# The length-64 sums of an inverse transform kept as unsplit 32-bit numbers, and their transposing product run on 32-bit operands

## The chip, the cores and the metric

The kernel runs on one core of a Trainium2 chip. The metric is device time in microseconds (us) of one execution. The time before is the median of 3 runs. Engines are called PE (TensorE), PEld (the weight loads of TensorE, a row of its own in the profile), DVE (VectorE), ACT (ScalarE), POOL (GpSimd) and SP (SyncE, which issues most DMAs).

## The reference

```python
X = np.fft.rfft(x, axis=1)                       # x: 8 x 2496 x 256, 32-bit
Yr = Xr @ w_r - Xi @ w_i + b_r                   # w: 256 x 256
Yi = Xr @ w_i + Xi @ w_r + b_i
Y  = sign(Y) * max(abs(Y) - 0.01, 0)             # real and imaginary part each
y  = np.fft.irfft(Y, n=2496, axis=1)             # 8 x 2496 x 256
...
logits = y @ w_gate + modality_bias[modality_id] # 8 experts, the largest logit takes the token
out = gate_w * (relu(y @ w1[e]) @ w2[e])         # w1: 256 x 1024, w2: 1024 x 256
```

The 8 batches of 2496 rows are 19968 tokens for the second part. Everything is 32-bit in and out.

## The kernel before

The length 2496 is written as 39 times 64. The forward transform sums over 39 (function s1), passes through DRAM, sums over 64 (s2), multiplies by the weights (mix), shrinks, and the inverse sums over 64 (is2) and then over 39 (is1). A batch has 10 **pairs** p of frequency indices k1; one pair is the work of s2, mix, shrink and is2 for two k1. After its 10 pairs a batch has 22 **pivots** j. A pivot takes three of the 64 positions, 120 columns (3 positions x 20 k1 x real and imaginary), and with TensorE turns channels-on-partitions into frequencies-on-partitions; the same product makes the gate logits, because its moving operand holds the identity (128 columns) and 16 columns of gate weights. is1 then sums over 39 and leaves the tokens in a tile x1, from which indirect DMAs (scatter, issued by POOL) sort them by expert. When all batches are done, the expert layers run tile by tile to the end.

TensorE is given operands of the kind fp32r throughout: a 32-bit number is rounded to a shorter one (hi), the rest is kept as a second one (lo), and a product is written as a sum of products of halves, for example hi*hi + lo*hi + hi*lo. So each value that TensorE reads later costs a rounding copy (ACT), a subtraction (DVE or POOL) and more than one product.

The order on PE, ACT, DVE and POOL is written out by hand: each engine executes its instructions in the order of the program text and waits at the head of its queue. In step p of a batch the text is: load and split for pair p+4 and p+3, s2 of pair p+2, mix and shrink of pair p+1, is2 of pair p, and one to three small steps of the routing of the batch before (lines 509 to 570, DVE above all). In the loop over j each step is: one scatter, one pivot, the is1 of the pivot two steps earlier, and in every other step one s1 chunk of the batch after the next (batches 0 to 5 only).

The names that matter: zh and zl (the sums over 64, hi and lo, one tile each for a whole batch), Zt (the difference before lo is made), pv (the moving operand of the pivot), ph and pl (the halves of what the pivot gives). In is2_pair there are two k1 per pair, and for each one ACT rounds into zh (line 380), DVE subtracts into Zt (line 381) and DVE adds the low part of the product into zl (line 389). PSUM tiles z_*, from which all three read, have two buffers; the tile of s2 has one, and DVE is its last reader (lines 314 and 315).

Of the kernel before, what the change touches and what calls it, by code (L numbers as in the profile page):

```python
# [9 lines left out]
F32 = mybir.dt.float32  # L10
F32R = mybir.dt.float32r
# [11 lines left out]
N1, N2, K1 = 39, 64, 20  # L23
D = 256
E = 8
# [5 lines left out]
PK = 3 * 2 * K1  # L31
# [96 lines left out]
class Attn:  # L128
# [65 lines left out]
    def consts_last(self):  # L194

        nc, I, cp = self.nc, self.I, self.cp
        st = self.w3.tile([128, 4 * D], F32, tag="ev", name="st_g")
        nc.sync.dma_start(st[:PK, :256], I["c_g"])
        ident = st[:, 256:384]
        nc.gpsimd.memset(ident, 0.0)  # L200
        nc.gpsimd.affine_select(out=ident, in_=ident, compare_op=ALU.not_equal, fill=1.0, base=0,
                                pattern=[[-1, 128]], channel_multiplier=1)
        gst = st[:, 384:384 + 2 * E].rearrange("p (c e) -> p c e", c=2)
        nc.sync.dma_start(gst, I["moe_w_gate"].rearrange("(c p) e -> p c e", p=128))
        yield
        self.g = self.cl.tile([PK, 2, 128], F32R, name="c_g")
        nc.vector.tensor_copy(self.g, st[:PK, :256].rearrange("p (h n) -> p h n", h=2))

        self.pv = self.cl.tile([128, 2, 144], F32R, name="pv")
        for c in range(2):  # L210
            io, go = (0, 128) if c == 0 else (16, 0)
            nc.vector.tensor_copy(self.pv[:, c, io:io + 128], ident)
            nc.vector.tensor_copy(self.pv[:, c, go:go + E], gst[:, c, :])
            nc.vector.tensor_sub(self.pv[:, c, go + E:go + 2 * E], gst[:, c, :], self.pv[:, c, go:go + E])


    def s1_load(self, b, u, end=None, eng=None):
# [144 lines left out]
    def is2_pair(self, b, p, parts):  # L362

        nc = self.nc
        if p == 0:
            self.zh = self.w1.tile([128, 2, N2, K1, 2], F32R, tag="zh", name=f"zh_{b}")
            self.zl = self.w1.tile([128, 2, N2, K1, 2], F32R, tag="zl", name=f"zl_{b}")
        out = []
        k1s = [(sh[:, i], sl[:, i]) for _, sh, sl in parts for i in range(sh.shape[1])]
        for i, (sh, sl) in enumerate(k1s):  # L370
            k1 = 2 * p + i
            ps = self.ps.tile([128, 2, 256], F32, tag="z", name=f"z_{b}_{k1}")
            mv = self.q[:, k1 * 256:(k1 + 1) * 256]
            for c in range(2):
                nc.tensor.matmul(ps[:, c, :], sh[:, c * 128:(c + 1) * 128], mv, start=True, stop=False)
                nc.tensor.matmul(ps[:, c, :], sl[:, c * 128:(c + 1) * 128], mv, start=False, stop=True)
            hv = ps[:, :, 0:128].rearrange("p c (n r) -> p c n r", r=2)
            lv = ps[:, :, 128:256].rearrange("p c (n r) -> p c n r", r=2)
            t = self.w2.tile([128, 2, N2, 2], F32, tag="Zt", name=f"Zt_{b}_{k1}")
            nc.scalar.copy(self.zh[:, :, :, k1, :], hv)  # L380
            nc.vector.tensor_sub(t, hv, self.zh[:, :, :, k1, :])
            out.append((k1, t, lv))
            if len(parts) > 1:
                self.z_low(*out.pop())
        for o in out:
            self.z_low(*o)

    def z_low(self, k1, t, lv):
        self.nc.vector.tensor_add(self.zl[:, :, :, k1, :], t, lv)


    def pivot(self, b, j):
        nc = self.nc
        base = min(3 * j, N2 - 3)
        tag = "y" if j % 2 and (j < 16 or b >= self.nb - 2) else "z"
        ps = self.ps.tile([128, 512], F32, tag=tag, name=f"pv_{b}_{j}")
        first = True
        for c in range(2):
            for z in (self.zh, self.zl):
                lhsT = z[:, c, base:base + 3, :, :].rearrange("p n k r -> p (n k r)")  # L400
                nc.tensor.matmul(ps[:PK, c * 128:c * 128 + 144], lhsT, self.pv[:, c, :],
                                 start=first, stop=(c == 1 and z is self.zl), skip_group_check=True)
                first = False
        ph = self.w2.tile([PK, GC], F32R, tag="ph", name=f"ph_{b}_{j}")
        pl = self.w2.tile([PK, GC], F32R, tag="pl", name=f"pl_{b}_{j}")
        nc.scalar.copy(ph, ps[:PK, :GC])  # L406
        nc.vector.tensor_sub(pl, ps[:PK, :GC], ph)  # L407
        return ph, pl
# [839 lines left out]
```

## Time and profile before

| | |
|---|---|
| time, median of 3 runs | 1660.69 us (1658.56 to 1667.56) |
| the profiled execution: time | 1657.9 us |
| its span from first to last instruction | 1656.1 us |
| mean granted TensorE clock | 0.979 of full speed |
| busy: PE / PEld / DVE / ACT / POOL | 1566.3 / 1522.0 / 900.6 / 792.0 / 638.0 us |
| pairs and pivots of all batches | until about 713 us |
| expert layers | from about 714 us to the end |

Busy time is a sum of the durations of one engine's instructions, where overlapping ones count once. Matmuls are pipelined: the duration of one (some 0.27 us) is longer than the distance to the next one, so what a product costs a full PE is read from the distance between two starts. A "[idle before <-releaser]" note names what the engine waited for last; where the named engine was done long before, it was another.

### The profile page before, as it was taken

The page shows a single profiled execution, that of the slowest core. Times are in us where ns is not written, and L with a number is a line of the kernel's source. Part 1 is how long each engine was busy: PE and PEld are TensorE (multiplying, and loading weights), DVE is VectorE, ACT ScalarE, POOL GpSimd, SP SyncE. Part 2 cuts the span into 40 slices and gives each one's busy share as a digit, 9 for nine tenths or more (in the row PEclk, how much of TensorE's full clock was granted, in tenths as well). Part 3 has the DMA queues.
Part 4 walks back from the last instruction along what each step waited for, and adds up shares of the span by engine and source line. Part 5 has one row for each costly group of instructions (what it writes and reads, how often), then busy time and mean ns, then how long its engine had stood idle before and what let it go on. Part 6 is the DMA issues. An engine that isn't in the chain of part 4 may idle for free. (4 is left out here: it accounts for less than half of the span.)

```text
span 1656.1 us, 34047 instructions
## 1 busy us (share of the span) xinstructions
PE 1566.3 (95%) x12771; PEld 1522.0 (92%) x12771; DVE 900.6 (54%) x1847; ACT 792.0 (48%) x1658; POOL 638.0 (39%) x601
## 2 busy tenths in 40 slices
PE   4899989899989999999999999999999999999998
PEld 2788888798888888899999999999999999999998
DVE  3988978797979797754333333333333333333332
ACT  3678877787778776642322332323222332232232
POOL 1563767676767677621531111111111111111111
PEclk7999999999999999999999999999999999999999
DMA  7757575757475746551341411641114117515240
GB/s 204 253 165 233 163 249 160 243 162 251 150 243 161 228 141 207 173 202 40 94 129 51 158 41 41 256 147 40 53 54 145 40 54 299 202 41 219 78 151 20
DMA packets 120462, 246.18 MB, mean 149 GB/s; under 512 B 18890, under 2 KB 74262, under 8 KB 116479
## 3 DMA queue, kind: packets, MB, share of 16 engines
q1 hardware_dynamic: 101305, 201.78, 37.5%
q0 software_dynamic: 18992, 42.22, 7.6%
q8 instruction: 102, 1.67, 0.4%
q14 instruction: 63, 0.52, 0.1%
HBM read 433.83 MB, written 100.82 MB: 323 GB/s over the span
## 5 line engine op out<-in xcount | busy, mean ns | idle before, releaser
L869 POOL DMA_INDIRECT out<-o,ix x161 | 158.6, 985 | 750.9 <-ACT o L848 699.4
L856 PE MATMUL y<-w,hh 128*128 128x256 f32 x2496 | 433.6, 278 | 0.0
L826 PE MATMUL h<-xh,w 128*128 128x256 f32 x2496 | 425.6, 283 | 0.9 <-ACT xh L805 0.7
L856 PEld LDWEIGHTS y<-w,hh 128*128 128x128 f32 x2496 | 378.0, 188 | 0.4
L826 PEld LDWEIGHTS h<-xh,w 128*128 128x128 f32 x2496 | 346.0, 189 | 1.2 <-ACT xh L805 0.9
L856 PE MATMUL y<-w,hl 128*128 128x256 f32 x1248 | 346.6, 278 | 0.0
L829 DVE SCALAR_TENSOR_TENSOR hl<-h,hh 128x512 fp32r<-128x512 f32 x312 | 215.8, 692 | 230.2 <-ACT hh L828 230.1
L828 ACT ACTIVATE hh<-h 128x512 fp32r<-128x512 f32 x312 | 186.5, 598 | 272.0 <-PE h L826 272.0
L826 PE MATMUL h<-xl,w 128*128 128x256 f32 x1248 | 247.3, 280 | 0.2 <-DVE xl L806 0.2
L856 PEld LDWEIGHTS y<-w,hl 128*128 128x128 f32 x1248 | 234.4, 188 | 0.0
L846 DVE TENSOR_SCALAR o<-y,xt 128x256 f32<-128x256 f32 x78 | 37.7, 484 | 342.9 <-ACT o L848 338.6
L848 ACT ACTIVATE o<-y,xt 128x256 f32<-128x256 f32 x78 | 37.0, 474 | 360.6 <-PE y L856 360.6
L575 POOL DMA_INDIRECT xs<-x,si x176 | 180.2, 1024 | 54.8 <-issue 52.1
L826 PEld LDWEIGHTS h<-xl,w 128*128 128x128 f32 x1248 | 191.1, 189 | 0.4 <-DVE xl L806 0.4
L346 PE MATMUL mx<-wmix,Xh 128*128 128x256 f32 x1280 | 175.9, 281 | 0.0
L346 PEld LDWEIGHTS mx<-wmix,Xh 128*128 128x128 f32 x1280 | 162.0, 191 | 0.8 <-ACT mx L326 0.2
L296 POOL TENSOR_TENSOR al<-a,ah 128x512 fp32r<-128x512 f32 x80 | 109.5, 1369 | 74.5 <-ACT ah L295 48.1
L360 POOL TENSOR_TENSOR sl<-s,sh 128x512 fp32r<-128x512 f32 x77 | 100.1, 1300 | 85.3 <-ACT sh L359 72.4
L307 PE MATMUL s<-c_m,ah 128*128 128x256 f32 x320 | 83.5, 295 | 29.7 <-DVE Xl L315 10.6
L407 DVE TENSOR_TENSOR pl<-pv,ph 120x272 fp32r<-120x272 f32 x176 | 76.8, 439 | 53.4 <-ACT ph L406 46.3
L346 PE MATMUL mx<-wmix,Xl 128*128 128x256 f32 x640 | 100.2, 279 | 0.0
L307 PEld LDWEIGHTS s<-c_m,ah 128*128 128x128 f32 x320 | 61.8, 193 | 37.1 <-ACT zh L380 12.3
(199 smaller groups left out, 2830.0 us busy)
## 6 DMA issues: line engine op xcount, KB each, us to landing
w<-wsp SPq DMA_DIRECT2D x166, 2048.0 KB
xt<-xs SPq DMA_DIRECT2D x78, 272.0 KB
a<-scr SPq DMA_DIRECT2D x80, 256.0 KB
scr<-ev SPq DMA_DIRECT2D x112, 160.0 KB
x<-in_x SPq DMA_DIRECT2D x108, 156.0 KB
wr<-in_moe_w SPq DMA_DIRECT2D x64, 256.0 KB
wsp<-wh SPq DMA_DIRECT2D x64, 256.0 KB
wsp<-wl SPq DMA_DIRECT2D x64, 256.0 KB
```

Source lines behind the costliest of these rows:

```text
L296: nc.gpsimd.tensor_sub(al, at, ah)
L307: nc.tensor.matmul(o, ah[:, i, c * 128:(c + 1) * 128], mv, start=True, stop=False)
L346: self.nc.tensor.matmul(ps[i][:, i, :], t[:, 2 * i + c, o:o + 128], self.w[:, wi, c, lo, :], start=False, stop=n == len(ops) - 1, skip_gro ...
L360: eng.tensor_sub(sl, s, sh)
L407: nc.vector.tensor_sub(pl, ps[:PK, :GC], ph)
L575: i = self.nc.gpsimd.indirect_dma_start(out=self.xs, out_offset=bass.IndirectOffsetOnAxis(ap=si[:, k:k + 1], axis=0), in_=self.at.x1[:, j, ...
L826: nc.tensor.matmul(ps[:, q, :], w1[:, lo, c, f * 128:(f + 1) * 128], x[:, c, :], start=n == 0, stop=n == 5)
L828: nc.scalar.activation(hh[:, 2 * p:2 * p + 2, :], ps, AF.Relu)
L829: nc.vector.scalar_tensor_tensor(hl[:, 2 * p:2 * p + 2, :], ps, 0.0, hh[:, 2 * p:2 * p + 2, :], ALU.max, ALU.subtract)
L846: nc.vector.tensor_scalar_mul(o[:, s, :], y[s], gate)
L856: nc.tensor.matmul(y[s], lhsT, w2[:, lo, f, :], start=n == 0, stop=n == 23)
L869: ins = self.nc.gpsimd.indirect_dma_start(out=self.out, out_offset=bass.IndirectOffsetOnAxis(ap=ix, axis=0), in_=o, in_offset=None, bounds ...
```

## The change

The sums over 64 are stored as one unsplit 32-bit tile z instead of zh and zl: ACT copies the high columns of the product, DVE adds the low columns in place. The pivot multiplies z and pv as 32-bit operands (F32 instead of F32R), two products per pivot instead of four. pv holds the gate weights unsplit, and the 8 columns that held their low parts hold zeros. What follows the pivot (ph, pl, is1) stays.

```diff
-        self.pv = self.cl.tile([128, 2, 144], F32R, name="pv")
+        self.pv = self.cl.tile([128, 2, 144], F32, name="pv")
+        nc.vector.memset(self.pv, 0.0)
         for c in range(2):
...
-            nc.vector.tensor_sub(self.pv[:, c, go + E:go + 2 * E], gst[:, c, :], self.pv[:, c, go:go + E])
...
         if p == 0:
-            self.zh = self.w1.tile([128, 2, N2, K1, 2], F32R, tag="zh", name=f"zh_{b}")
-            self.zl = self.w1.tile([128, 2, N2, K1, 2], F32R, tag="zl", name=f"zl_{b}")
-        out = []
+            self.z = self.w1.tile([128, 2, N2, K1, 2], F32, tag="zh", name=f"z_{b}")
...
-            t = self.w2.tile([128, 2, N2, 2], F32, tag="Zt", name=f"Zt_{b}_{k1}")
-            nc.scalar.copy(self.zh[:, :, :, k1, :], hv)
-            nc.vector.tensor_sub(t, hv, self.zh[:, :, :, k1, :])
-            out.append((k1, t, lv))
-            if len(parts) > 1:
-                self.z_low(*out.pop())
-        for o in out:
-            self.z_low(*o)
-
-    def z_low(self, k1, t, lv):
-        self.nc.vector.tensor_add(self.zl[:, :, :, k1, :], t, lv)
+            z = self.z[:, :, :, k1, :]
+            nc.scalar.copy(z, hv)
+            nc.vector.tensor_add(z, z, lv)
...
-        first = True
         for c in range(2):
-            for z in (self.zh, self.zl):
-                lhsT = z[:, c, base:base + 3, :, :].rearrange("p n k r -> p (n k r)")
-                nc.tensor.matmul(ps[:PK, c * 128:c * 128 + 144], lhsT, self.pv[:, c, :],
-                                 start=first, stop=(c == 1 and z is self.zl), skip_group_check=True)
-                first = False
+            lhsT = self.z[:, c, base:base + 3, :, :].rearrange("p n k r -> p (n k r)")
+            nc.tensor.matmul(ps[:PK, c * 128:c * 128 + 144], lhsT, self.pv[:, c, :],
+                             start=c == 0, stop=c == 1, skip_group_check=True)
```

## Rows read from the trace of the kernel before

**Rows 1.** The page: span, and busy time, share and instructions of each engine.

```profile
span 1656.1 us, 34047 instructions
PE 1566.3 (95%) x12771; PEld 1522.0 (92%) x12771; DVE 900.6 (54%) x1847; ACT 792.0 (48%) x1658; POOL 638.0 (39%) x601
```

**Rows 2.** Windows, pairs of batch 2 and sum over batches 1 to 7: busy, clock, DMA.

```profile
226.00:282.00 56.00, 51.35 (x420) 49.46 (x421) 51.09 (x105) 45.10 (x98) 39.90 (x35) 1.00 0.57 179
...
sum 369.50, PE 343.94 PEld 332.70 DVE 334.02 ACT 296.49 POOL 258.89; mean PE 49.13 PEld 47.53 DVE 47.72 ACT 42.36 POOL 36.98
```

**Rows 3.** Windows, pivot loops of batches 0, 4 and 7 (of 8): the same columns.

```profile
117.50:143.50 26.00, 24.58 (x182) 22.67 (x183) 21.10 (x45) 21.46 (x56) 0.92 (x1) 1.00 0.70 223
...
447.00:479.00 32.00, 27.51 (x177) 24.92 (x178) 22.42 (x47) 22.09 (x54) 21.55 (x21) 0.90 0.79 236
...
691.00:712.50 21.50, 20.39 (x150) 20.01 (x149) 10.53 (x25) 13.88 (x41) 16.99 (x21) 0.84 0.47 146
```

**Rows 4.** Groups by line of what the change touches: count, busy us, mean ns.

```profile
L401 PE MATMUL pv<-pv,zl 128*120 128x144 f32 x352 | 90.3, 285 | 0.5 <-DVE zl L389 0.5
L401 PE MATMUL pv<-pv,zh 128*120 128x144 f32 x352 | 84.8, 268 | 11.1 <-DVE zl L389 9.0 <-DVE pl L407 1.2 <-ACT u L354 0.9
...
L381 DVE TENSOR_TENSOR Zt<-z,zh 128x256 f32<-128x256 f32 x160 | 59.8, 413 | 1.3
L389 DVE TENSOR_TENSOR zl<-Zt,z 128x256 fp32r<-128x256 f32 x160 | 59.5, 413 | 0.1
```

**Rows 5.** Timeline of PE in batch 0's pivot loop: start, duration.

```profile
121.18 0.40 PE L270 MATMUL s<-x1h,c_f 117*120 117x512 f32 x1
121.41 0.39 PE L271 MATMUL s<-x1l,c_f 117*120 117x512 f32 x1
121.64 0.23 PE L401 MATMUL pv<-pv,zh 128*120 128x144 f32 x1
121.71 0.27 PE L401 MATMUL pv<-pv,zl 128*120 128x144 f32 x1
121.81 0.27 PE L401 MATMUL pv<-pv,zh 128*120 128x144 f32 x1
121.92 0.27 PE L401 MATMUL pv<-pv,zl 128*120 128x144 f32 x1
122.03 0.32 PE L413 MATMUL i<-ph,c_g 120*117 120x272 f32 x1
122.19 0.29 PE L414 MATMUL i<-ph,c_g 120*117 120x272 f32 x1
122.31 0.29 PE L415 MATMUL i<-pl,c_g 120*117 120x272 f32 x1
```

**Rows 6.** Timeline of PEld, pairs of batch 2: every stop within the stretch.

```profile
236.56 0.19 PEld L307 LDWEIGHTS s<-c_m,ah 128*128 128x128 f32 x1 [1.72 <-ACT wh L1000]
...
241.81 0.19 PEld L307 LDWEIGHTS s<-c_m,ah 128*128 128x128 f32 x1 [0.47 <-ACT u L354]
...
247.19 0.19 PEld L307 LDWEIGHTS s<-c_m,ah 128*128 128x128 f32 x1 [0.30 <-issue]
...
257.99 0.19 PEld L307 LDWEIGHTS s<-c_m,ah 128*128 128x128 f32 x1 [1.22 <-ACT zh L380]
...
272.45 0.19 PEld L307 LDWEIGHTS s<-c_m,ah 128*128 128x128 f32 x1 [0.19 <-ACT u L354]
...
280.24 0.18 PEld L401 LDWEIGHTS pv<-pv,zh 128*120 128x120 f32 x1 [2.01 <-ACT sh L359]
```

**Rows 7.** Timeline of DVE around the first stop of Rows 6.

```profile
231.45 0.76 DVE L381 TENSOR_TENSOR Zt<-z,zh 128x256 f32<-128x256 f32 x2
232.12 0.75 DVE L389 TENSOR_TENSOR zl<-Zt,z 128x256 fp32r<-128x256 f32 x2
...
235.76 0.69 DVE L315 TENSOR_TENSOR Xl<-Xt,s 128x512 fp32r<-128x512 f32 x1
```

**Rows 8.** Waits of PE in batch 2's pivot loop: us in total, times, longest.

```profile
PE i L413 <- ACT x L416: 3.4, 2, 2.6
```

## The prediction

> **What bounds the kernel now.** I read the page first [rows 1]: PE is busy for 95% of the span, and DVE, ACT and POOL for about half or less. That is an average over two halves. From about 714 us the expert layers run, where PE has no stop and nothing of this change occurs; I cost that half at nothing. The chain of waits of this execution ends in the small conditional block after the last tile and shows only its last microsecond, so the first half is read by stages.
>
> The windows come second. In the pairs [rows 2] DVE is busy for 334.0 of 369.5 us and PEld for 332.7: two engines at 90%, with ACT at 80%. In the pivot loops [rows 3] PE leads alone: in batch 0 it is busy for 24.6 of 26.0 us, in batch 7 for 20.4 of 21.5. The six loops between take longer for the same PE work (batch 4: 32.0 us with 27.5 busy, some of that at a lower clock), because scatters and loads of x come in; batch 6 has no s1, but routing in its place.
>
> Third, the timelines. In the pairs PE stops a few times per batch [rows 6], and what it waits for is DVE, although the notes name ACT: the first stop ends at 236.56, just after DVE's Xl that began at 235.76 and took 0.69 us [rows 7]. That is the last reader of the one PSUM tile of s2. The longest stop, 2.01 us ahead of the first pivot, is the same lateness: the pivot needs the last zl. So the change takes work from the engine that makes PE late in the pairs, and puts work on PE where PE is the bound.
>
> **What the change removes: one of two DVE operations per k1.** 160 subtractions L381 go, 59.8 us of busy time [rows 4]. Two adjacent ones hold DVE for 0.67 us (231.45 to 232.12 [rows 7]). The add that remains reads z where it read Zt; it is one operation of 256 elements with one operand from PSUM, as L389 was, and I keep its 413 ns. The ACT copy of equal size stays as it is.
>
> What that gives PE: DVE has a few pauses left (51.1 of 56.0 us busy [rows 2]), after each of which its lateness starts anew. I therefore take off one pair's saving, 0.67 us, of a stop within the pairs, and all of it if it is shorter. In batch 2 [rows 6] that is 0.67 + 0.47 + 0.30 + 0.67 + 0.19 = 2.30 us. Ahead of the first pivot lateness of the pair before counts, and the last pair's own subtractions go too; I take off two pairs' worth, 1.34 of 2.01 us. Together 3.64 us per batch, for the six stages of batches 1 to 6 21.8 us. For the stages of batch 0 (start-up waits on loads) and batch 7 (no s2 at its end) I take half each, 3.6 together: 25.4 us. Then the next engine shows: ACT is at 42.4 us per stage [rows 2], against 400 products of 256 columns on PE, 46 us at 0.45 ns per column (below), and it is unevenly loaded, since six of the ten pairs also split expert weights. I give back 0.6 us for each of seven stages: 21 us remain. Bounds: 0 if ACT takes over at once, 41 us (seven times 5.9) if no stop remains.
>
> **What it adds: 32-bit products.** Before, a pivot is four fp32r products of 144 columns; their starts are 0.07, 0.10, 0.11 and 0.11 us apart, 0.39 us in sum [rows 5]. Columns alone would need less: 512 columns take 0.23 us, 0.45 ns each, so 144 take 0.065, which is the first step; the other three run at the pace of the loads of 120 weight columns, 0.105 us.
>
> No row shows a product on 32-bit operands that isn't a transposition. Bounds from the nearest rows: at least one fp32r product (0.105 us, 0.21 per pivot, 31.7 us gained over 176 pivots); at most what the kernel would write for a full product of two split operands, hi*hi, hi*lo, lo*hi and lo*lo (it writes three of them in L413 to L415), each with its load: 4 x 0.105 = 0.42 us, 0.84 per pivot, 79 us lost. Between these I take four streams of the columns with the loads of both weight halves hidden under them: two loads are 0.21 us, and 4 x 144 = 576 columns at 0.45 ns are 0.26 us. I choose it because both halves of the moving operand can run over one set of weights, so a second load of the same half buys nothing. A pivot then takes 0.52 us, 0.13 more than before, and 176 pivots 22.9 us more.
>
> The Trainium skill (FP8 and Floating Point Precision, section TensorE Precision Notes) says the same of the number: true FP32 goes through the array in 4 passes, H*H + H*L + L*H + L*L. It speaks against the change, since "two products instead of four" is eight passes instead of four; by it the sum is 0.52 or 0.84 us per pivot, as the loads are shared or not, and no run here shows which yet.
>
> How much of the 22.9 us meets the path: all in batches 0 and 7 (2.9 us each), where PE is the bound [rows 3]. In the other six loops PE also waits for tokens and x rows, for example 3.4 us in two waits in batch 2 [rows 8]; such a wait shrinks when PE arrives later. I hide 1.2 of 2.9 us in each, 7 us in all, and 15.9 us remain.
>
> **What moves besides.** The clock: in the loops of batches 4 and 7 it is granted at 0.90 and 0.84 of 2.4 GHz on the mean [rows 3], so there are stretches at 1.2 GHz; 32 us at 0.90 and 21.5 us at 0.84 are 3.2 and 3.4 us of lost speed, some 3 us a loop. With fewer stops ahead of these loops and more columns in them I expect a part back and take 4 us (0 to 9). The pv edits are one small memset for two small subtractions, once; DVE has them beside the pairs of batch 0. No load and no place in a queue changes. Pivots that come later make x1 later; is1 runs two pivots behind, which covers it.
>
> **Sum.** +15.9 - 21 - 4 = -9.1 us on the profiled execution's 1657.9 us (span 1656.1). The median of the runs is 2.8 us above that execution, so against 1660.7 the forecast is 1651.6 us. What a measurement of this kernel can tell from no change is about 0.5%, 8.3 us, so it is just on the border of "faster". Its own range is 1636 (cost 12, gain 30, clock 7) to 1671 (cost 23, gain 13, clock 0).
>
> **The rivals.**
>
> *The weights are loaded for each of the four parts.* A product then costs 0.42 us and the pivot loop of a batch 22 x 0.45 = 9.9 us more. That is 79 us less the 7 hidden, less 21 gained in the pairs, no clock back: +51, 1712 us. For it: three of four products of today's pivot run at the load's pace and not at the columns' [rows 5]. Against it: there are only two different halves to load. It decides from 0.29 us per product on: there 176 x (0.58 - 0.39) = 33 us are as much as hiding, gain and clock together (7 + 21 + 4). This is the case on the other side; I give it 0.25.
>
> *The pairs don't get shorter.* ACT, or POOL's sl, sets their pace once DVE is relieved, and only the 1.34 us ahead of seven pivot loops (9 us) are gained: 15.9 - 9 = +7, 1668 us. For it: ACT at 80%; against it: the stops end with DVE's Xl. Chance 0.08.
>
> *The 32-bit product streams only twice.* Then the two loads bind, 0.21 us each product, 0.42 per pivot: +5 us, less 21 and 4: 1641 us. For it: nothing but that no row excludes it. Chance 0.10.
>
> The forecast keeps 0.57. It falls to faster in 0.31, to no change in 0.23 and to slower in 0.03; the second rival to no change in 0.05 and slower in 0.03. Faster: 0.31 + 0.10 = 0.41; the same: 0.23 + 0.05 = 0.28; slower: 0.25 + 0.03 + 0.03 = 0.31. The range runs from 1634 to 1712: it leaves out about half of the first rival and the low tail, some 0.16.
>
> **What would show it.** Right: pivots in batch 0 whose two products start 0.26 us apart; loops of batches 0 and 7 longer by about 3 us, the others by less; DVE at about 41 us per stage in the pairs; stops ahead of s2 of 0.5 to 1 us at most, and under 1 us ahead of the first pivot. Wrong: products 0.4 us apart (then the loops grow by 10 us each), or unchanged stops in the pairs with DVE idle before them, or loops of batches 1 to 6 that grow by the full 3 us or more, which would say that their waits move along with PE.

## The result, and the profile after

The changed kernel takes 1647.21 us (median of six runs, 1644.38 to 1650.02), the kernel before 1659.68 us beside it (median of six). The ratio is 0.9918 [0.9896, 0.9940]: faster by 0.8%, 12.5 us, where 1651.6 us was forecast. The profiled execution of after is the slowest of its six, 1650.02 us with a span of 1648.3, so the two traces differ by only 7.8 us.

The page of after: span, and busy time, share and instructions of each engine.

```profile
span 1648.3 us, 33821 instructions
PE 1571.4 (95%) x12771; PEld 1522.8 (92%) x12771; DVE 863.8 (52%) x1686; ACT 790.8 (48%) x1658; POOL 644.0 (39%) x601
```

DVE has lost 36.8 us and 161 instructions against [rows 1]. The subtractions came in 80 twos, which at 0.67 us [rows 7] are 53.6 us in sum, but other operations took longer: those of L317, which make part of Xl and last between 0.29 and 1.42 us each in both traces, came to 51.4 us instead of 42.8. Why they did was not looked into. PE executes as many matmuls as before, 12771, although 352 products were taken out of the text. The groups of after by line tell why (count, busy us, mean ns).

```profile
L389 PE MATMUL pv<-pv,z 128*120 128x144 f32 x704 | 116.4, 290 | 6.6 <-DVE z L379 5.3 <-DVE pl L394 1.1
L379 DVE TENSOR_TENSOR z<-z,z 128x256 f32<-128x256 f32 x160 | 59.8, 415 | 2.0 <-ACT z L378 0.5
```

352 products on 32-bit operands stand in the trace as 704 matmuls, two for each. The addition that remains costs what L389 did [rows 4].

Next the stages. "Pairs" are the stretches from a batch's last pivot to the next batch's first one, batches 1 to 7; "loops" run from a batch's first pivot to its last. The first fence gives before's sums with these exact borders, pairs and then loops; the second gives after's pairs of batch 2 and their sum; the third after's loops of batches 0, 2, 4 and 7 and their sum. Columns are as in [rows 2].

```profile
sum 380.35, PE 349.66 PEld 338.24 DVE 342.56 ACT 303.36 POOL 263.67; mean PE 49.95 PEld 48.32 DVE 48.94 ACT 43.34 POOL 37.67
...
sum 214.51, PE 196.48 PEld 180.09 DVE 146.01 ACT 149.01 POOL 139.54; mean PE 24.56 PEld 22.51 DVE 18.25 ACT 18.63 POOL 17.44
```

```profile
227.21:280.61 53.40, 51.06 (x421) 49.19 (x420) 45.71 (x84) 43.84 (x95) 38.12 (x33) 1.00 0.56 179
...
sum 369.19, PE 350.76 PEld 338.50 DVE 312.46 ACT 300.50 POOL 260.73; mean PE 50.11 PEld 48.36 DVE 44.64 ACT 42.93 POOL 37.25
```

```profile
118.51:144.46 25.95, 25.34 (x174) 23.21 (x175) 20.88 (x43) 21.13 (x53) 1.28 (x1) 1.00 0.70 217
...
280.61:309.49 28.88, 26.87 (x174) 23.51 (x175) 19.17 (x41) 20.80 (x52) 22.13 (x20) 1.00 0.83 255
...
444.14:472.38 28.24, 26.30 (x174) 23.41 (x175) 19.01 (x40) 20.26 (x51) 21.46 (x20) 1.00 0.82 248
...
683.71:701.98 18.27, 18.27 (x147) 18.27 (x148) 9.00 (x21) 13.29 (x39) 14.38 (x18) 1.00 0.52 155
sum 214.28, PE 197.87 PEld 178.79 DVE 144.72 ACT 151.10 POOL 147.26; mean PE 24.73 PEld 22.35 DVE 18.09 ACT 18.89 POOL 18.41
```

The account between the two traces: the first pivot starts 1.0 us later, the pairs are 11.2 us shorter, the loops 0.2, so the last pivot ends 10.4 us earlier (701.98 against 712.41); the expert layers after it give 2.6 us back (946.3 against 943.7). What stands out is the loops: dearer pivots, and no longer loops. The granted clock is part of that: batches 4 and 7 ran at 0.90 and 0.84 [rows 3] and run at 1.00 now. Length times (1 - granted clock), summed over the eight loops, was 18.4 us before and is 1.6 now.

The timeline of PE in batch 0's loop after (start, duration), where [rows 5] stand for before.

```profile
121.61 0.65 PE L389 MATMUL pv<-pv,z 128*120 128x144 f32 x4
122.01 0.38 PE L400 MATMUL i<-ph,c_g 120*117 120x272 f32 x1
122.23 0.29 PE L401 MATMUL i<-ph,c_g 120*117 120x272 f32 x1
122.35 0.29 PE L402 MATMUL i<-pl,c_g 120*117 120x272 f32 x1
122.48 0.40 PE L269 MATMUL s<-x1h,c_f 117*120 117x512 f32 x1
```

The row of four matmuls spans 0.65 us and one lasts 0.286, so they start (0.65 - 0.286) / 3 = 0.12 us apart. A pivot and its is1 together take 0.87 us (121.61 to 122.48); before it was 0.79 (from one pivot's start at 704.71 to the next one's at 705.50). That is 0.08 more where 0.13 was forecast.

Last, PEld's stops in the pairs of batch 2, all above 0.5 us and one smaller, for [rows 6].

```profile
239.25 0.99 PEld L346 LDWEIGHTS mx<-wmix,Xh 128*128 128x128 f32 x8 [0.86 <-ACT mx L326]
...
243.34 0.19 PEld L307 LDWEIGHTS s<-c_m,ah 128*128 128x128 f32 x1 [0.37 <-ACT u L354]
...
263.72 0.19 PEld L307 LDWEIGHTS s<-c_m,ah 128*128 128x128 f32 x1 [0.59 <-ACT mx L326]
...
280.61 1.02 PEld L389 LDWEIGHTS pv<-pv,z 128*120 128x120 f32 x8 [1.20 <-DVE z L379]
```

The stops of 1.72 and 1.22 us ahead of s2 are gone, the one ahead of the first pivot fell from 2.01 to 1.20, and a new one stands ahead of mix, 0.86 us, behind ACT.

PE's waits from 140 to 640 us, which hold six of the seven stretches of pairs, show the same in sum (us in total, times, longest). First before, then after:

```profile
PE s L307 <- DVE Xl L315: 9.6, 9, 1.6
...
PE pv L401 <- DVE zl L389: 7.6, 5, 1.6
...
PE s L307 <- ACT zh L380: 4.5, 4, 1.3
```

```profile
PE pv L389 <- DVE z L379: 4.1, 5, 0.9
PE mx L346 <- ACT mx L326: 3.6, 3, 1.8
...
PE s L307 <- ACT z L378: 1.2, 2, 0.6
PE s L307 <- DVE Xl L315: 1.2, 4, 0.4
```

The three waits of before, 21.7 us, have shrunk to 6.5, and the one ahead of mix takes 3.6 of that back.

### The profile page after: what moved, and what is told of

The parts are those of the page before. It is cut to its first block, busy times and chain, and to the rows that moved or that the text cites. A ratio compares the mean times of both kernels' runs of the same rounds, so it can differ in the third digit from the quotient of the medians.

```text
span 1648.3 us, 33821 instructions
## 1 busy us (share of the span) xinstructions
PE 1571.4 (95%) x12771; PEld 1522.8 (92%) x12771; DVE 863.8 (52%) x1686; ACT 790.8 (48%) x1658; POOL 644.0 (39%) x601
## 5 line engine op out<-in xcount | busy, mean ns | idle before, releaser
L562 POOL DMA_INDIRECT xs<-x,si x176 | 186.2, 1058 | 54.0 <-issue 51.7
L389 PE MATMUL pv<-pv,z 128*120 128x144 f32 x704 | 116.4, 290 | 6.6 <-DVE z L379 5.3
L389 PEld LDWEIGHTS pv<-pv,z 128*120 128x120 f32 x704 | 100.2, 184 | 17.6 <-DVE z L379 8.5
```

The source lines that it names most:

```text
L562: i = self.nc.gpsimd.indirect_dma_start(out=self.xs, out_offset=bass.IndirectOffsetOnAxis(ap=si[:, k:k + 1], axis=0), in_=self.at.x1[:, j, ...
```

## The experiments

Times are medians; "loops" and "pairs" are the sums defined above, "lost" is length times (1 - granted clock) over the eight loops, each from one profiled execution. Diffs are against the changed kernel where nothing else is said. Each group had the kernel before beside it, on the same chip: e1 to e4 a median of 1658.95 us, e5 to e8 1659.62, e11 and e12 1658.11. On the chip of e9 and e10 the kernel before took 1761.08 us. A sum of pairs or loops from one trace is a rough measure: the same kernel (after and e12_again) has pairs of 369.2 and 368.4 us, and e5_wide and e7_four_f32, whose edits touch nothing in the pairs, have 363.9 and 362.8. A difference of some 3 us in the pairs is therefore not shown to come from an edit to them.

| kernel | us | against before | pairs | loops | lost |
|---|---|---|---|---|---|
| before | 1659.68 | | 380.4 | 214.5 | 18.4 |
| after | 1647.21 | 0.9918 [0.9896, 0.9940] | 369.2 | 214.3 | 1.6 |
| e1_no_sub | 1646.51 | 0.9925 [0.9901, 0.9949] | 364.9 | 217.4 | 12.7 |
| e2_idle_sub | 1663.38 | 1.0019 [0.9998, 1.0041] | 385.2 | 216.7 | 6.6 |
| e3_two_fp32r | 1650.63 | 0.9934 [0.9914, 0.9955] | 371.1 | 211.1 | 24.8 |
| e4_two_wh | 1646.20 | 0.9908 [0.9883, 0.9933] | 366.5 | 218.0 | 2.2 |
| e5_wide | 1696.49 | one run | 363.9 | 269.6 | 1.5 |
| e6_five_fp32r | 1663.99 | 1.0020 [0.9997, 1.0043] | 367.2 | 219.4 | 3.3 |
| e7_four_f32 | 1694.35 | 1.0208 [1.0189, 1.0228] | 362.8 | 270.5 | 0.0 |
| e8_scatter_ahead | 1646.97 | 0.9925 [0.9904, 0.9946] | 372.8 | 207.3 | 0.0 |
| e9_both (other chip) | 1733.30 | 0.9860 [0.9828, 0.9892] | 369.4 | 284.2 | 46.7 |
| e10_again (other chip) | 1740.01 | 0.9889 [0.9857, 0.9922] | 366.1 | 291.6 | 53 |
| e11_both_again | 1641.45 | 0.9909 [0.9884, 0.9935] | 369.7 | 204.1 | 0.0 |
| e12_again | 1645.61 | 0.9927 [0.9907, 0.9947] | 368.4 | 214.9 | 3.6 |

**The subtraction taken out alone (e1_no_sub).** The four fp32r products of before stay, zl is the low part alone. The diff is against the kernel before.

```diff
+        self.zero = cp.tile([128, 2, N2, 2], F32, name="zero")
+        nc.vector.memset(self.zero, 0.0)
...
-            t = self.w2.tile([128, 2, N2, 2], F32, tag="Zt", name=f"Zt_{b}_{k1}")
             nc.scalar.copy(self.zh[:, :, :, k1, :], hv)
-            nc.vector.tensor_sub(t, hv, self.zh[:, :, :, k1, :])
-            out.append((k1, t, lv))
+            out.append((k1, self.zero, lv))
```

> The kernel before without the 160 subtractions Zt: zl gets the low columns of the product plus a tile of zeros, so the remainder of rounding zh is left out. The pivots keep four fp32r products. Theory (DVE's lateness is what the change takes away, the 32-bit products are a cost): the pairs of batches 1 to 7 become as short as with the whole change, about 11 us in sum, the pivot loops stay as before; ahead of the changed kernel by the price of its pivots, so 1640 to 1647 us. Rival (the gain comes from the pivots, whose first product no longer waits for two tiles, or from a clock that denser pivots keep up): no gain, 1655 to 1662 us.

**The subtraction put back (e2_idle_sub).** The changed kernel with one subtraction per k1 whose result nobody reads.

```diff
             nc.scalar.copy(z, hv)
+            t = self.w2.tile([128, 2, N2, 2], F32, tag="Zt", name=f"Zt_{b}_{k1}")
+            nc.vector.tensor_sub(t, hv, z)
+            out.append((z, lv))
...
             nc.vector.tensor_add(z, z, lv)
```

> The changed kernel with an idle subtraction per k1 put back on DVE, in the old place and of the old size, whose result nobody reads; pivots on 32-bit operands. Theory: stops in the pairs come back, DVE is at 47 to 48 us per stage again, and the pivots cost 0.07 us each more than before, so 1658 to 1668 us, not faster than the kernel before. Rival (the pivots or the clock give the gain): 1645 to 1652 us, as the changed kernel.

The sums over the pairs, first without the subtraction, then with the idle one.

```profile
sum 364.92, PE 349.75 PEld 338.08 DVE 310.87 ACT 298.54 POOL 259.76; mean PE 49.96 PEld 48.30 DVE 44.41 ACT 42.65 POOL 37.11
```

```profile
sum 385.21, PE 349.16 PEld 337.39 DVE 344.73 ACT 304.28 POOL 267.40; mean PE 49.88 PEld 48.20 DVE 49.25 ACT 43.47 POOL 38.20
```

DVE's 310.9 and 344.7 us of busy time go with pairs of 364.9 and 385.2 us, while PE's busy time is the same within 0.6 us. Taking the subtraction out of the kernel before gives 12.4 us (1646.51 against 1658.95); putting it back into the changed one costs 16.2 (1663.38 against 1647.21). Both times lie in the theory's range. e1_no_sub and after, with the same number of operations on DVE, differ in the pivots and what they read, and end 0.7 us apart; so do e2_idle_sub and before, 4.4 us apart, with an interval that reaches to no difference. Nor is it the clock: e2_idle_sub loses 6.6 us to it in its loops where before lost 18.4, and is no faster, with loops 2.2 us longer. So the gain comes from the work taken off DVE; the 32-bit pivots cost the run between nothing and some 5 us. Why the idle subtraction makes the pairs 4.9 us longer than before's was not followed up.

**Pivots at half the price (e3_two_fp32r).** z and pv become fp32r, two products per pivot without the low halves.

```diff
-        self.pv = self.cl.tile([128, 2, 144], F32, name="pv")
-        nc.vector.memset(self.pv, 0.0)
+        self.pv = self.cl.tile([128, 2, 144], F32R, name="pv")
+        nc.vector.memset(self.pv.bitcast(F32), 0.0)
...
-            self.z = self.w1.tile([128, 2, N2, K1, 2], F32, tag="zh", name=f"z_{b}")
+            self.z = self.w1.tile([128, 2, N2, K1, 2], F32R, tag="zh", name=f"z_{b}")
```

> The changed kernel with z and pv as fp32r: two products of one pass per pivot; the low halves of the sums and of the gate weights are left out. A pivot of 0.21 us in place of 0.46. Theory (PE is the bound of a pivot loop only in batches 0 and 7; the loops of batches 1 to 6 are held by tokens, x rows and DMA): 5 us gained in each of those two loops and 0 to 3 us in each of the others, 1625 to 1638 us. Rival (PE is the bound in all loops): 176 x 0.25 = 44 us, about 1603 us. Rival (no loop cares): 1647 us.

It missed: 1650.63 us, no faster than with 32-bit products, nearest to the rival in which no loop cares. Its loops of batches 2, 4 and 6:

```profile
281.71:309.67 27.96, 22.61 (x130) 17.91 (x130) 18.89 (x40) 20.93 (x52) 22.54 (x20) 1.00 0.81 261
...
445.60:474.42 28.82, 24.24 (x130) 20.01 (x130) 19.70 (x41) 21.04 (x52) 21.68 (x20) 0.88 0.80 250
...
606.99:632.87 25.88, 21.30 (x102) 19.41 (x103) 18.32 (x61) 13.86 (x36) 20.30 (x21) 0.66 0.61 197
```

Batch 2 ran at the full clock in both kernels: PE is busy 4.3 us less than in after (22.61 against 26.87) and the loop is 0.9 us shorter. So PE doesn't set the length of this loop. In other loops the clock is granted at 0.88 and 0.66, and the clock of its nine runs, 0.969 to 0.973 on the mean of each, is below that of every run of after (0.985 to 0.989). In batch 0, which has a full clock and no scatters, the loop is 0.8 us shorter (25.19) with PE busy 20.85 us: PE stops there once for 2.7 us, behind DVE's pl, while ACT waits 1.9 us ahead of wh for the store of an earlier one (wsp<-wh). Batch 7's is 1.4 us shorter (16.88), at a clock of 0.80.

**The price of one product.** First the moving operand is widened from 144 to 288 columns (e5_wide), then each product is made twice (e7_four_f32).

```diff
-        self.pv = self.cl.tile([128, 2, 144], F32, name="pv")
+        self.pv = self.cl.tile([128, 2, 288], F32, name="pv")
...
-            nc.tensor.matmul(ps[:PK, c * 128:c * 128 + 144], lhsT, self.pv[:, c, :],
+            nc.tensor.matmul(ps[:PK, c * 128:c * 128 + 288], lhsT, self.pv[:, c, :],
```

> The changed kernel with the pivot's moving operand widened from 144 to 288 columns; the added columns hold zeros and land behind what is read. It measures what sets the price of a 32-bit product, which the profile shows as two loads and two products. Theory (the columns set it: each of the two runs two streams of 144 columns at 0.42 ns, 0.12 us): the distance between two of the four doubles to about 0.24 us and a pivot takes 0.94 us. Rival (the two loads of 120 weight columns set it, 0.105 us or a little more): the distance stays at 0.12 us until the columns catch up, 288 columns in one stream.

```diff
-        for c in range(2):
+        for c in (0, 1, 0, 1):
```

> The changed kernel with each pivot's two 32-bit products made twice, the second time over the first: 0.92 us per pivot. Theory (the loops of batches 0, 6 and 7 are set by PE, those of batches 1 to 5 by POOL's chain of scatters, 20 times 1.35 us, with 2 to 3 us of slack on PE): batches 0, 6 and 7 grow by 8 to 10 us each, batches 1 to 5 by 5 to 8 us each, some 55 to 65 us in all, 1700 to 1712 us. Rival (PE has no slack anywhere): 176 x 0.46 = 81 us, 1728 us. Rival (POOL alone sets the middle loops): under 35 us, below 1682 us.

The timeline of PE with 288 columns, batch 0:

```profile
125.43 1.13 PE L389 MATMUL pv<-pv,z 128*120 128x288 f32 x4
126.19 0.51 PE L400 MATMUL i<-ph,c_g 120*117 120x272 f32 x1
```

The windows of the loops with four products, batches 0, 4 and 7:

```profile
115.80:151.18 35.38, 35.38 (x262) 33.99 (x263) 21.26 (x43) 22.13 (x53) 1.28 (x1) 1.00 0.58 180
...
467.46:502.84 35.38, 35.38 (x262) 33.99 (x263) 21.37 (x42) 21.70 (x52) 21.52 (x20) 1.00 0.77 224
...
719.94:749.03 29.09, 29.09 (x235) 29.09 (x236) 9.28 (x21) 13.57 (x40) 16.41 (x21) 1.00 0.55 188
```

With twice the columns four matmuls span 1.13 us instead of 0.65, the first product after the pivot starts 0.76 us behind it instead of 0.40: the columns set the price, not the loads. With two products more, PE is busy through the whole of every loop, and batch 7's, in which after too has PE busy throughout, grows by 29.09 - 18.27 = 10.82 us; by 22 pivots and two products that is 0.246 us for a product of 144 columns. (The loops grew by 56.2 us, as the theory had it, but the run came in at 1694.35 us, under its range, since the pairs are 6.4 us shorter and the rest of the run some 6 us.) It also tells what PE needs alone in the loops of batches 0 to 5: 35.38 - 22 x 0.49 = 24.6 us. In after they take 25.95 (batch 0) and 27.8 to 29.9 us (batches 1 to 5).

**A fifth fp32r product per pivot (e6_five_fp32r).** e1_no_sub with one more product, later overwritten. The diff is against e1_no_sub.

```diff
+        lhsT = self.zh[:, 0, base:base + 3, :, :].rearrange("p n k r -> p (n k r)")
+        nc.tensor.matmul(ps[:PK, 0:144], lhsT, self.pv[:, 0, :], start=True, stop=False, skip_group_check=True)
```

> The kernel before without the subtractions Zt (the remainder of rounding zh is left out, as in e1_no_sub) and with a fifth fp32r product per pivot, whose result the next one overwrites: 0.49 us per pivot, about what a pivot on 32-bit operands takes. It asks why the changed kernel loses hardly any speed to the clock in its pivot loops (1.6 us, against 12.7 in e1_no_sub and 18.4 before). Theory (PE's busy time in the loop decides, whatever the operands): clock of the span 0.986 to 0.990, loss in the loops under 5 us. Rival (it is the 32-bit operands, which keep the array at work through the whole pivot while fp32r products wait for their loads): clock 0.981 to 0.986 as e1_no_sub, loss in the loops 8 to 15 us. Time 1642 to 1652 us by either.

Inconclusive. The median is 1663.99 us, 12 us above the range, but the runs go from 1649.46 to 1670.16, and the profiled one, with 3.3 us lost in the loops and a mean clock of 0.987, is the fastest; the run of 1653.34 us had 0.986, and the five others, 1661 to 1670 us, 0.971 to 0.976. So in this kernel a lower clock goes with 10 us or more; but more work on PE brought the higher clock in two runs of seven only, so that the dearer pivots of after are what keeps its clock up stays unproven.

**What holds the loops of batches 1 to 6.** In after, ACT's copies of x wait for scatters. The first fence is ACT's waits from 140 to 640 us (us in total, times, longest), the second the timeline of POOL in batch 2's loop, its first scatter and the last ones.

```profile
ACT x L403 <- DMA xs<-x,si: 29.2, 27, 2.7
...
ACT wh L987 <- DMA wsp<-wh: 9.6, 7, 3.0
```

```profile
280.63 1.02 POOL L562 DMA_INDIRECT xs<-x,si  x1 [0.19 <-issue]
...
299.26 0.99 POOL L562 DMA_INDIRECT xs<-x,si  x1 [0.30 <-issue]
300.56 0.99 POOL L562 DMA_INDIRECT xs<-x,si  x1 [0.30 <-issue]
301.86 0.99 POOL L562 DMA_INDIRECT xs<-x,si  x1 [0.30 <-issue]
303.15 0.99 POOL L562 DMA_INDIRECT xs<-x,si  x1 [0.30 <-PE i L402]
...
307.15 0.99 POOL L562 DMA_INDIRECT xs<-x,si  x1 [0.30 <-issue]
```

The scatters at the end start 1.30 us apart; others in this loop take up to 1.47 us each instead of 0.99. In the trace 19 scatters and one sl (line 360), POOL's other operation there, fill this loop from 280.63 to 308.14 us, 27.5 of 28.9 us, with pauses of 0.30 us at most. In batches 1 to 5 this row is 26.9 to 28.4 us long, more than the 24.6 us that PE needs. (The expectation of e7_four_f32 counts 20 scatters; one of the 20 operations is sl.) The x tile that ACT fills comes free when its scatter has read it. So in the program text two scatters of each loop were moved into the pairs (e8_scatter_ahead):

```diff
-                        rt.scatter((0, 8, 8)[p - 7] if done else (1, 2, 3)[p - 7])
+                        rt.scatter((0, 8, 8)[p - 7] if done else (1, 3, 4)[p - 7])
```

> The changed kernel with two more scatters ahead of each pivot loop: (1, 3, 4) at pairs 7, 8 and 9 in place of (1, 2, 3). Theory (POOL's chain of scatters sets the loops of batches 1 to 5): each is one or two scatters of 1.3 us shorter, 6 to 12 us in sum, 1636 to 1642 us, unless POOL is then late with the low halves that PE needs in the last pairs. Rival (PE, ACT or DMA set the loops): 1645 to 1650 us, loops unchanged.

The sums of pairs and of loops with the scatters ahead:

```profile
sum 372.82, PE 352.45 PEld 339.95 DVE 307.11 ACT 301.56 POOL 264.34; mean PE 50.35 PEld 48.56 DVE 43.87 ACT 43.08 POOL 37.76
```

```profile
sum 207.27, PE 194.06 PEld 176.18 DVE 145.26 ACT 149.51 POOL 137.63; mean PE 24.26 PEld 22.02 DVE 18.16 ACT 18.69 POOL 17.20
```

In the trace one scatter has left the loops of batches 1 to 5 and two that of batch 6, since those of pair 9 run beside the first pivots. The loops are 7.0 us shorter with the pivots unchanged (of batches 1 to 6 only batch 3's is longer, by 1.1), and 1.6 of this can be clock that came back. ACT's copies of x wait 7.1 us for scatters where they waited 29.2. So the scatters are a good part of what holds the loops. But the pairs are 3.6 us longer, with a new wait of PE: POOL, held by the scatters, is late with the low half sl. The median is that of after, 1646.97 us, and the expected gain did not come. ACT's and PE's waits from 140 to 640 us:

```profile
ACT x L403 <- DMA xs<-x,si: 7.1, 10, 1.6
...
PE z L374 <- POOL sl L360: 6.4, 6, 2.0
```

In after that last wait was 0.7 us.

**What holds the pairs now.** The waits above show ACT standing 9.6 us in seven waits before it can round expert weights into wh. The timeline of after in batch 5's pairs shows what is late then:

```profile
484.96 0.62 ACT L987 CAST wh<-wr 128x512 fp32r<-128x512 f32 x1 [3.01 <-DMA wsp<-wh]
...
486.07 0.59 ACT L326 COPY mx<-bias 128x512 f32<-128x512 f32 x1
...
486.71 1.08 PE L346 MATMUL mx<-wmix,Xh 128*128 128x256 f32 x7 [1.83 <-ACT mx L326]
```

The wait is for the store of the last wh (wsp<-wh), out of the single buffer of that tile. Waiting for it is not new: before, ACT stood 4.1 us for the stores of wh and 4.6 for those of wl in the same stretch (140 to 640 us), but PE had no stop ahead of mix then. The edit (e4_two_wh) gives wh and wl two, and to make room for them the tile of batch 1's x rows is cut to the part that is used.

```diff
-                self.early = self.w1.tile([128, 2, N2, K1, 2], F32R, tag="zl" if b else "zh", name=f"x_{b}")
...
+                    self.early = self.w1.tile([128, 12 * D], F32, tag="zl", name=f"x_{b}")
...
-            sw = SplitWeights(tc, I, at.w2, at.w1, wsp)
+            sw = SplitWeights(tc, I, at.w2, at.w2, wsp)
```

> The changed kernel with two buffers for the halves of the expert weights (wh, wl), for which the tile of batch 1's x rows is cut to the 12 KB that are used. Theory (the new stop of PE before mix, 4.4 us in four stops, is ACT standing at wh until a store has left its only buffer): these stops go and the pairs get 3 to 5 us shorter, 1642 to 1645 us. Rival (the next late operation takes their place, or the earlier stores are in the way of other DMAs): 1646 to 1650 us.

This wait of ACT and PE's stop ahead of mix are gone from the lists, and the pairs are 2.7 us shorter (366.5), no more than the pairs vary by without an edit to them. The loops are 3.8 longer (218.0), the copies of x wait 33.7 us for scatters instead of 29.2, and the median, 1646.20 us, is that of after within the intervals: the rival's range.

**Both together.** Each edit removes one wait, and in its trace another stage is longer. So both were made, beside the changed kernel again; first on the other chip.

> The changed kernel with both edits that shortened one part of it: two buffers for wh and wl (e4_two_wh: pairs 366.5 in place of 369.2 us) and two more scatters ahead of each loop (e8_scatter_ahead: loops 207.3 in place of 214.3 us). If the parts add up: 1637 to 1642 us. If what one part gains the other gives back (POOL's scatters in the last pairs stand before the low halves that PE needs, and the clock falls again): 1644 to 1648 us, as each alone.

> The changed kernel once more, beside e9_both on the same chip: 1644 to 1650 us. By the theory that the pivots on 32-bit operands cost next to nothing in the loops, its loops are again within 3 us of the 214.5 us of before and lose under 5 us to the clock, and its pairs are 11 to 15 us shorter than the 380.4 us of before.

> The kernel of e9_both again, because its first run fell on a chip on which the kernel before took 1761 us. If the parts add up: 1637 to 1642 us against 1659 us of before, a ratio of 0.987 to 0.990. If one gives back what the other gains: 1644 to 1648 us.

> The changed kernel again beside it, 1644 to 1650 us against 1659 us of before; pivot loops within 3 us of 214.5 us in sum, pairs of batches 1 to 7 11 to 15 us shorter than 380.4 us.

On the other chip neither time came out as expected: 1733.30 and 1740.01 us, with loops of 284.2 and 291.6 us where 214.5 was expected, and pairs of 369.4 and 366.1. Beside the last kernel before, after came out as expected in time, loops and pairs (e12_again). With both edits the loops take 204.1 us, 10.8 less than in e12_again, and the pairs 369.7. 1641.45 us is the lowest median of the study, 4.2 us under after beside it, but the intervals against the kernel before, [0.9884, 0.9935] and [0.9907, 0.9947], overlap, and its six runs fall into two groups, 1637.0 to 1638.6 and 1644.3 to 1648.1 us, of which the profiled one is the fastest: it beats the kernel before, and over the changed kernel its gain is not shown. PE's waits up to 715 us have the one behind POOL again, where the scatters went:

```profile
PE z L378 <- POOL sl L364: 6.3, 6, 2.0
```

## Why the prediction was right, point by point

- **The pairs get shorter because DVE gets lighter: right, at about half to three quarters of the size.** The term was -21 us; the trace shows -11.2, that of e12_again -12.0, e1_no_sub -15.5 in the pairs and -12.4 in its time. The stops ahead of s2 went as forecast. Three assumptions were off. The stop before the first pivot came to 1.20 us where less than 1 was forecast. The new stop ahead of mix, up to 2.0 us long, was not foreseen (4.4 us in four waits of PEld, 140 to 640 us): ACT was taken to cost 0.6 us a stage for its busy time, and what it costs is a wait for the store of wh, which no busy share shows and which stood in ACT's waits of before already. And DVE's 41 us per stage didn't follow from the prediction's own working: ten pairs at 0.67 us off 51.1 are 44.4, and 45.7 was measured, as other operations of DVE took longer.
- **The price of a product: right.** Forecast 0.26 us, four streams of the columns with the loads hidden; measured 0.246, which is 4 x 144 columns at 0.43 ns, and the columns set it (e5_wide, e7_four_f32). The Trainium skill's four passes for true FP32 (FP8 and Floating Point Precision, section TensorE Precision Notes) agree with that number. The rival with a load for every part would have needed 0.42, the one with two streams 0.21; both are out.
- **The price of a pivot: too high.** Forecast +0.13 us, measured +0.08 for a pivot with its is1 (0.87 against 0.79), some 14 us for 176 pivots instead of 22.9. The pivot's start to the is1's is 0.40 us, as it was (0.39, [rows 5]); the difference shows only in the first is1 product, 0.22 us instead of 0.16.
- **How much of it meets the path: the step that failed.** +15.9 us was forecast, after hiding 7; together with the clock's -4 the loops should have grown by 12. They are 0.2 us shorter. Batch 0's grew by 1.0 (24.95 to 25.95) and not 2.9; batch 7's fell by 2.2 (20.50 to 18.27) with the clock back at 1.00. The hiding was sized by 3.4 us of PE's own waits in one loop [rows 8]. What it left out is that the loops of batches 1 to 5 are longer than PE needs (24.6 us, e7_four_f32), that POOL's row of scatters alone takes 26.9 to 28.4 us there, and that the loops move with it (e8_scatter_ahead): PE waits less when it has more to do. In batch 2 of e3_two_fp32r 4.3 us less of PE gave 0.9 us. One loop showed the prediction's sign of being wrong: batch 1's, at the full clock in both traces, grew by 3.1 us (26.71 to 29.85). But with the old pivots it is as long (29.10 in e1_no_sub), so it is not their price; POOL's row in it grew from 26.3 to 27.3 us.
- **The clock: right in sign, under-sized.** 4 us (0 to 9) were to come back; 16.8 us less are lost in the loops of the two traces. How much of this shortened the run is open: in batch 7, where PE is busy throughout, it did; in loops that PE doesn't set, a lower clock may fill time in which PE would have waited; in e2_idle_sub 11.8 us less were lost than before and the loops were no shorter. Nor is it shown why it came back: the kernel with less PE work in the pivots has the lowest clock (e3_two_fp32r), but e6_five_fp32r, meant to test that, came out both ways.
- **The sum.** +15.9 - 21 - 4 was the forecast. The trace has -0.2 for loops and clock together, -11.2 for the pairs, +1.0 ahead of the first pivot and +2.6 around the first expert tiles, where 1.7 us of clock are lost (0.94 in the 28 us after the last pivot): -7.8. So the forecast was close partly by luck: a gain of 21 and a cost of 15.9 were both taken too large, and the errors nearly cancel. The two traces differ by less than the medians do (12.5 us), since the profiled execution of after is its slowest.

## What to carry to other kernels

A pass that saves work on one engine is worth what the stops behind that engine are worth, less the wait that is next in line; look for it in the timeline as a wait for a buffer or a store, not in busy shares. An operand left in 32 bits trades a rounding copy's companion subtraction and a second tile against four streams of the columns, which is nearly the price of four split products here (0.49 against 0.39 us); it paid because the engine that splits was the late one. Before costing more matmul work in a loop, find out what the loop takes with that work doubled and halved: a busy PE at 93% need not be what sets its length.

## What the runs showed of the hardware

- A 32-bit product of 120 weight columns and 144 moving columns stands in the trace as two weight loads and two matmuls, 0.12 us apart, 0.246 us in all; with 288 columns the matmuls are about 0.24 us apart, (1.13 - 0.40) / 3.
- The kernel with half the matmul work in its pivots was granted the lowest clock (0.969 to 0.973 on the mean of a run), the one with each product made twice the highest (0.990 to 0.992), and after stands between (0.985 to 0.990 in its twelve runs on the faster chips). The five fp32r products break the order: 0.971 to 0.987.
- An indirect scatter issued by POOL recurred every 1.30 us at the shortest, 0.99 us busy and 0.30 us idle (after, batch 2), and some took up to 1.47 us.
- On one chip the same kernels took 1733 to 1761 us. There the profile of e10_again shows PE standing in the loops with no releaser to be seen; such stops of PEld between 140 and 640 us are 33.0 us in sum there and 4.9 in after. PE's waits of e10_again over its whole span, us in total, times, longest:

```profile
PE i L400 <- issue: 42.0, 22, 4.3
```

Its loops lost 53 us to the clock. What it waited for was not found.
